# Spreading the weight loads over the first attention pairs, and storing the last tokens in pieces

## Chip, cores, metric

The kernel runs on one core of a Trainium2 chip. The metric is the device time of one execution in microseconds (us). Engines are named as in the profile: PE is TensorE (matmuls; PEld its weight loads), DVE is VectorE, ACT ScalarE, POOL GpSimd, SP SyncE. A name with a q (SPq, POOLq, ACTq) is the queue from which an engine issues DMAs.

## The reference

Attention without a mask, and behind it a two-layer MLP with a leaky ReLU, on 8 batches of 12 heads, 448 tokens of 64 numbers each:

```python
scores = scale * np.matmul(q, k.transpose(0, 1, 3, 2))
attn = np.exp(scores - max); attn = attn / np.sum(attn, axis=-1)
x = np.matmul(attn, v).transpose(0, 2, 1, 3).reshape(3584, 768)
h = x @ w_in            # 768 x 2048
out = np.maximum(0.01 * h, h) @ w_out   # 2048 x 768
```

Inputs and output are float32; the kernel multiplies in bf16.

## The kernel before

**Units.** Two heads of one batch make a pair; there are 48 pairs, six for a batch. For each pair `load` (line 97) brings q, k and v from memory by three DMAs on SP's queue (224 KB each), and `cast` (lines 108 to 110) turns them to bf16, on POOL for all pairs but the first. `transposes` turns q and k so that the head dimension lies on partitions: eight PE matmuls against an identity (line 169) and one DVE copy (line 172). For pairs from `NPE` = 12 on `dma_transposes` does it by a DMA transpose on SP (line 157). `scores(u, c)` multiplies q with a quarter of the keys (line 181) for both heads, `expo` takes the exponential on ACT (line 190), and `pv(u, j)` multiplies with v for one head (line 199); v has a column of ones, so the sum comes along, and DVE divides (lines 206 and 207) into `x`. `x_transposes` turns x into `xT`, on PE (lines 220 and 221) for pairs below 9 and by a DMA transpose from pair 9 on.

**MLP tiles.** Tokens are cut at multiples of 128 into eight tiles, one ending at or below the end of each batch: tile 0 has 384 tokens, others 384 or 512. `mlp(i)` is a generator of groups. First 16 groups of six matmuls each with w_in (line 250), each evicted by ACT with a leaky ReLU (line 254). Then two groups for each 128 tokens, one for each half of 384 columns, of 16 matmuls with w_out (line 268), evicted by a DVE copy into `o` (line 272). When the second half is done, `store` writes 128 rows by two DMAs on SP (line 232); they are two since rows of the output are interleaved by four in a batch.

**Order.** The order is written out by hand, and each engine runs its instructions in it. `first(u)` is the step of one of the first six pairs: scores and exponentials of pair u, heads of pair u - 1, transposes of pair u + 1, cast of pair u + 3, load of pair u + 5. From then on attention goes in clusters of three score quarters with what belongs to them (`cluster(g)`), put between groups of the MLP by `catch_up`. In tile 0 that is by the share of columns done; cluster 8, the first, goes ahead of all groups. Tile i waits for the attention of its own batch.

**Weights.** `load_w` issues w_in and w_out from POOL's queue in four pieces each (line 123), a DMA that also converts to bf16. The first piece of w_in is issued behind the casts of pair 0, ahead of those of pairs 1 and 2; the others from `first(2)` on:

```python
load_w({2: 1, 3: 2, 4: 2, 5: 2}.get(u, 0))
```

**Buffers.** PSUM has three score buffers of two banks (`ps_s`) and two others (`ps_g`) that transposes, heads and MLP groups share. Raw loads have five buffers, casts four. Each DMA of SP's queue waits for the landing of the one issued eight before it.

Of the kernel before, what the change touches and what calls it, by code (L numbers as in the profile page):

```python
# [9 lines left out]
F32 = mybir.dt.float32  # L10
BF16 = mybir.dt.bfloat16
# [5 lines left out]
def kernel(  # L17
# [53 lines left out]
    NQ = 4  # L71
# [31 lines left out]
    def cast(u, by=(nc.gpsimd.tensor_copy,) * 3):  # L103
        if u >= NU:
            return
        fq, fk, fv = raw.pop(u)
        qk_sb[u] = cast_pool.tile([SC, 2, NSC, 2, D], BF16, name="qkb")
        by[0](qk_sb[u][:, 0].rearrange("p so h d -> p h so d"), fq)  # L108
        by[1](qk_sb[u][:, 1].rearrange("p so h d -> p h so d"), fk)  # L109
        by[2](v_sb[u % NV][:, :, :, :D], fv)  # L110
# [21 lines left out]
    def warm_up(n):  # L132
        for _ in range(n):
            ps = ps_g.tile([P, 512], F32, name="mm", tag="g")
            nc.tensor.matmul(ps, warm[:, :P], warm, start=True, stop=True)  # L135
# [19 lines left out]

    def turn(dst, src):
        nc.sync.dma_start_transpose(out=dst.rearrange("p (c s) -> p c s", s=SC), in_=src)
# [5 lines left out]
    def transposes(u):  # L163
        if u >= min(NPE, NU):
            return
        tr = ps_g.tile([P, 2, S], BF16, name="tr", tag="g")
        for i in range(2):
            for so in range(NSC):
                nc.tensor.transpose(  # L169
                    tr[:, i, ts(so, SC)], qk_sb[u][:, i, so], ident[:SC, :SC]  # L170
                )
        nc.vector.tensor_copy(qkT[u % NQ][:, :QL], tr.rearrange("p i s -> p (i s)"))  # L172

    sc_t = {}

    def scores(u, c):
        ps = ps_s.tile([P, 2, 512], F32, name="sc")
        t = qkT[u % NQ]
        sc_t[u, c] = ps
        for j in range(2):  # L180
            nc.tensor.matmul(  # L181
                ps[:, j, :S],
                t[j * D:(j + 1) * D, S + c * SC:S + c * SC + P],
                t[j * D:(j + 1) * D, :S],
                start=True, stop=True,
            )
# [24 lines left out]
    def x_transposes(u):  # L211
        b, hp = divmod(u, HP)
        at = b * S % NX
        dst = xT[:, hp, at:at + S]
        if u >= NPE - 3:
            turn(dst, x_t.pop(u).rearrange("p so h d -> p (so h d)"))
            return
        tr = ps_g.tile([P, 2, S], BF16, name="tr", tag="g")
# [5 lines left out]
    def store(o, t0):  # L224
# [17 lines left out]
    def mlp(i):  # L242

        n = cuts[i + 1] - cuts[i]
        at = cuts[i] % NX
        h = h_pool.tile([P, MD, 4 * P], BF16, name="h")
        for m in range(MD):
            ps = ps_g.tile([P, 4 * P], F32, name="mm", tag="g")
            for kk in range(KD):
                nc.tensor.matmul(  # L250
                    ps[:, :n], w_in_sb[:, kk, ts(m, P)], xT[:, kk, at:at + n],
                    start=(kk == 0), stop=(kk == KD - 1),
                )
# [4 lines left out]
        todo = [(c, w) for c in range(n // P) for w in range(2)]  # L258
        if i == 0:
            todo.sort(key=lambda cw: cw[1])  # L260
        o = {}
        for c, w in todo:
            settle()
            if c not in o:
                o[c] = o_pool.tile([P, DM], F32, name="o")
            ps = ps_g.tile([P, 4 * P], F32, name="mm", tag="g")
            for m in range(MD):
                nc.tensor.matmul(  # L268
                    ps[:, :NW], h[:, m, ts(c, P)], w_out_sb[:, m, ts(w, NW)],
                    start=(m == 0), stop=(m == MD - 1),  # L270
                )
            nc.vector.tensor_copy(o[c][:, ts(w, NW)], ps[:, :NW])  # L272
            if w == 1:
                store(o.pop(c), cuts[i] + c * P)
            yield MD * NW


    def first(u):

        scores(u, 0)  # L280
        scores(u, 1)
        expo(u, 0)
        if u == 0:
            warm_up(4)
        expo(u, 1)
        if u >= 2:
            x_transposes(u - 2)
        if u >= 1:
            pv(u - 1, 0)
        load(u + 5)  # L290
        load_w({2: 1, 3: 2, 4: 2, 5: 2}.get(u, 0))
        if u + 1 < HP:
            transposes(u + 1)
        scores(u, 2)
        scores(u, 3)
        expo(u, 2)
        expo(u, 3)
        cast(u + 3)
        if u >= 1:
            pv(u - 1, 1)  # L300


    def cluster(g):
        t, r = divmod(g, 4)
        u = 3 * t
        chunks = [divmod(4 * u + 3 * r + x, NSC) for x in range(3)]
        chunks = [(a, c) for a, c in chunks if a < NU]
        heads = [[(u - 1, 0)], [(u - 1, 1)], [(u, 0), (u, 1)], [(u + 1, 0), (u + 1, 1)]][r]
        heads = [(a, j) for a, j in heads if HP <= a < NU]
        turned = {0: u - 2, 2: u - 1, 3: u}.get(r)  # L310
        if turned is not None and HP <= turned < NPE - 3:
            x_transposes(turned)
        if len(heads) > 1:
            pv(*heads.pop(0))
        for a, c in chunks:
            scores(a, c)
        for a, c in chunks[:2]:
            expo(a, c)
        late.extend(chunks[2:])
        for a, j in heads:  # L320
            pv(a, j)
            if j == 1 and a >= NPE - 3:
# [12 lines left out]
    u = HP - 1  # L335
    pv(u, 0)
    x_transposes(u - 1)
    pv(u, 1)
    transposes(HP)
    x_transposes(u)  # L340


    begin = [8 * (i + 1) + 3 for i in range(B)]
    begin[0] = 8
    for i in range(B):
        work = list(range(begin[i], begin[i + 1])) if i + 1 < B else []
        n = cuts[i + 1] - cuts[i]
        total = MD * KD * n + n // P * MD * DM
        used, done = 0, 0
        lead = 1 if i == 0 else 0  # L350

        def catch_up():
            nonlocal done
            while done < len(work) and used * (len(work) - lead) >= total * (done + 1 - lead):
                settle()
                cluster(work[done])
                done += 1

        catch_up()
        for step in mlp(i):  # L360
            used += step
            catch_up()


# [28 lines left out]
```

The softmax here doesn't subtract the row's maximum and nothing guards it: scores larger than these inputs give would overflow.

## Time and profile before

| | |
|---|---|
| median of 11 runs | 426.0 us (423.9 to 428.72) |
| the profiled execution | 425.32 us, span 423.5 us |
| PE / ACT / DVE / POOL busy | 96% / 54% / 24% / 21% |
| DMA, mean | 150 GB/s, 63.66 MB |
| mean granted clock of PE | 0.994 |

The span runs from the first to the last instruction; the execution has 1.8 us around it. Busy shares are means over stages that differ: the first six pairs, where there is no MLP work yet, the seven tiles with attention between their groups, and the last tile alone. Times in the views are in us from the start of the span. "Idle before, releaser" in brackets at the end of a line is how long the engine stood before that instruction and whom it waited for.

### The profile page before, as it was taken

The page shows a single profiled execution, that of the slowest core. Times are in us where ns is not written, and L with a number is a line of the kernel's source. Part 1 is how long each engine was busy: PE and PEld are TensorE (multiplying, and loading weights), DVE is VectorE, ACT ScalarE, POOL GpSimd, SP SyncE. Part 2 cuts the span into 40 slices and gives each one's busy share as a digit, 9 for nine tenths or more (in the row PEclk, how much of TensorE's full clock was granted, in tenths as well). Part 3 has the DMA queues.
Part 4 walks back from the last instruction along what each step waited for, and adds up shares of the span by engine and source line. Part 5 has one row for each costly group of instructions (what it writes and reads, how often), then busy time and mean ns, then how long its engine had stood idle before and what let it go on. Part 6 is the DMA issues. An engine that isn't in the chain of part 4 may idle for free.

```text
span 423.5 us, 9000 instructions
## 1 busy us (share of the span) xinstructions
PE 408.4 (96%) x3731; PEld 234.3 (55%) x3731; DVE 99.7 (24%) x271; ACT 228.3 (54%) x322; POOL 91.0 (21%) x168
## 2 busy tenths in 40 slices
PE   8979999979999999999999999999999999999995
PEld 3645556544556656554565656654465666654562
DVE  1642323310132212221132212321032211320021
ACT  4957664556724684467634486456652577214200
POOL 5494320530311211131131213131120200000000
PEclk9989999999999999999999999999999999999999
DMA  9999999994465947777465785759275420230022
GB/s 225 259 249 245 249 250 217 248 231 99 105 161 155 208 111 184 185 155 178 97 153 146 199 146 132 198 155 208 60 171 149 118 56 15 58 86 2 0 76 74
DMA packets 98505, 63.66 MB, mean 150 GB/s; under 512 B 55456, under 2 KB 94880, under 8 KB 98464
## 3 DMA queue, kind: packets, MB, share of 16 engines
q1 hardware_dynamic: 90928, 56.56, 55.7%
q0 software_dynamic: 7296, 6.29, 9.2%
q8 instruction: 29, 0.48, 0.5%
q10 hardware_dynamic: 240, 0.23, 0.2%
q14 instruction: 12, 0.10, 0.1%
HBM read 45.61 MB, written 11.01 MB: 134 GB/s over the span
## 4 chain that ended last, share of the span: by engine, by line
PE 90%; DMA 6%; DVE 1%; SPq 1%; ACT 1%; POOL 0%; issue 0%; ACTq 0%
PE mm L250 34%; PE mm L268 34%; PE pv L199 12%; PE sc L181 9%; DMA fv<-in_v_dram 3%; DMA xT<-x 2%; DMA fq<-in_q_dram 1%; DVE o L272 1%; SPq L97 1%; DVE x L207 1%; PE tr L169 0%; ACT e L190 0%; DVE rec L206 0%; POOL w_in_sb L123 0%; SPq L232 0%
## 5 line engine op out<-in xcount | busy, mean ns | idle before, releaser
L190 ACT ACTIVATE e<-sc 112x896 bf16<-112x896 f32 x192 | 164.4, 918 | 104.7 <-PE sc L181 104.3
L250 PE MATMUL mm<-xT,w_in_sb 128*128 128x384 bf16 (+1 forms) x768 | 150.4, 353 | 2.9 <-DMA xT<-x 2.2
L268 PE MATMUL mm<-w_out_sb,h 128*128 128x384 bf16 x896 | 150.5, 326 | 0.6 <-DVE x L207 0.3
L268 PEld LDWEIGHTS <-h 128*128 128x128 bf16 x896 | 85.8, 98 | 55.4 <-DVE x L207 0.5
L250 PEld LDWEIGHTS <-w_in_sb 128*128 128x128 bf16 x768 | 72.9, 98 | 68.8 <-issue 2.7
L254 ACT ACTIVATE h<-mm 128x384 bf16<-128x384 f32 (+1 forms) x128 | 69.6, 544 | 61.9 <-PE mm L250 61.8
L110 POOL CAST v<-fv 112x512 bf16<-112x512 f32 x48 | 29.6, 616 | 209.1 <-PE pv L199 189.1
L199 PEld LDWEIGHTS <-e 112*128 112x128 bf16 x1536 | 57.1, 98 | 30.2 <-issue 17.9
L199 PE MATMUL pv<-v,e 112*128 112x65 bf16 x1536 | 66.4, 195 | 2.6 <-ACT e L190 1.2
L272 DVE COPY o<-mm 128x384 f32<-128x384 f32 x56 | 31.2, 558 | 133.7 <-PE mm L268 133.7
L206 DVE RECIPROCAL rec<-pv 112x4 f32<-112x4 f32 x96 | 17.5, 183 | 160.5 <-PE pv L199 160.4
L181 PE MATMUL sc<-qkT 64*128 64x448 bf16 x384 | 49.5, 357 | 0.7 <-DVE qkT L172 0.4
L207 DVE TENSOR_TENSOR x<-pv,rec 112x256 bf16<-112x256 f32 x96 | 40.8, 425 | 3.3
L108 POOL CAST qkb<-fq 112x512 bf16<-112x512 f32 x47 | 28.9, 615 | 26.2 <-DMA qkT<-qkb 12.7
L109 POOL CAST qkb<-fk 112x512 bf16<-112x512 f32 x47 | 28.9, 614 | 10.0 <-DMA fk<-in_k_dram 9.9
L181 PEld LDWEIGHTS <-qkT 64*128 64x128 bf16 x384 | 13.6, 94 | 19.5 <-issue 10.4
L172 DVE COPY qkT<-tr 128x896 bf16<-128x896 bf16 x12 | 7.4, 619 | 10.6 <-PE tr L169 10.6
L169 PE MATMUL tr<-ident,qkb 112*128 112x112 bf16 x96 | 7.6, 223 | 1.5 <-POOL qkb L108 1.4
L169 PEld LDWEIGHTS <-qkb 112*128 112x128 bf16 x96 | 5.6, 102 | 3.7 <-POOL qkb L108 1.7
L135 PE MATMUL mm<-warm 128*128 128x512 bf16 x15 | 5.8, 531 | 1.2 <-DVE warm L130 1.2
L221 DVE COPY xT<-tr 128x448 bf16<-128x448 bf16 x9 | 3.5, 389 | 7.2 <-PE tr L220 7.2
L220 PE MATMUL tr<-ident,x 112*128 112x112 bf16 x36 | 3.3, 214 | 0.5 <-DVE x L207 0.3
(17 smaller groups left out, 14.9 us busy)
## 6 DMA issues: line engine op xcount, KB each, us to landing
fq<-in_q_dram SPq DMA_DIRECT2D x48, 224.0 KB, 3.8
fv<-in_v_dram SPq DMA_DIRECT2D x48, 224.0 KB, 4.4
fk<-in_k_dram SPq DMA_DIRECT2D x47, 224.0 KB, 3.9
w_in_sb<-in_moe_w_in_dram POOLq DMA_DIRECT2D x4, 768.0 KB, 15.0
w_out_sb<-in_moe_w_out_dram POOLq DMA_DIRECT2D x4, 768.0 KB, 34.9
out_dram<-o SPq DMA_DIRECT2D x8, 336.0 KB, 3.1
out_dram<-o SPq DMA_DIRECT2D x8, 288.0 KB, 2.6
out_dram<-o SPq DMA_DIRECT2D x8, 240.0 KB, 3.4
```

What stands on the lines that cost most here:

```text
L108: by[0](qk_sb[u][:, 0].rearrange("p so h d -> p h so d"), fq)
L109: by[1](qk_sb[u][:, 1].rearrange("p so h d -> p h so d"), fk)
L110: by[2](v_sb[u % NV][:, :, :, :D], fv)
L181: nc.tensor.matmul(ps[:, j, :S], t[j * D:(j + 1) * D, S + c * SC:S + c * SC + P], t[j * D:(j + 1) * D, :S], start=True, stop=True,)
L190: nc.scalar.activation(e[:, :, c, :], sc_t.pop((u, c))[:SC, :, :S], AX.Exp, scale=scale)
L199: nc.tensor.matmul(ps[:, qc, :], e[:, at:at + P], vt[:, j, c, :], start=(c == 0), stop=(c == NSC - 1),)
L206: nc.vector.reciprocal(rec, ps[:SC, :, D:])
L207: nc.vector.tensor_mul(x_t[u][:, :, j, :], ps[:SC, :, :D], rec.to_broadcast([SC, NSC, D]))
L250: nc.tensor.matmul(ps[:, :n], w_in_sb[:, kk, ts(m, P)], xT[:, kk, at:at + n], start=(kk == 0), stop=(kk == KD - 1),)
L254: nc.scalar.activation(h[:, m, :n], ps[:, :n], AX.Prelu, alpha=0.01)
L268: nc.tensor.matmul(ps[:, :NW], h[:, m, ts(c, P)], w_out_sb[:, m, ts(w, NW)], start=(m == 0), stop=(m == MD - 1),)
L272: nc.vector.tensor_copy(o[c][:, ts(w, NW)], ps[:, :NW])
```

## The change

In the order of the code:

- The first piece of w_in is no longer issued ahead of pair 1's casts; `first(0)` to `first(5)` issue 1, 1, 1, 2, 2 and 1 pieces.
- k of pair 0 is cast in two halves, by ACT and POOL. For pair 0, `transposes` uses a tile and a DVE copy for q and one for k. The two warm-up matmuls behind them are taken out.
- `NPE` is 14: pairs 12 and 13 are turned on PE as well. The border for x stays at pair 9, with a name of its own, `NXP`.
- In a cluster, PE's transposes of q and k stand ahead of the scores instead of at the end, and in such a cluster no head is put ahead of the scores. x's transposes on PE stand behind the exponentials.
- After pair 5, the transposes of x (pairs 4 and 5) and of pair 6 use score buffers, and those of pair 4 come ahead of pair 5's heads.
- In tile 0 the eleven clusters come after 2, 4, ... 22 groups.
- In the last tile, the last group is made as two of 192 columns, and the last 128 tokens are stored after each of their three column pieces, 16 rows from ACT's queue and 112 from SP's.

```diff
-    cast(0, (nc.vector.tensor_copy, nc.scalar.copy, nc.gpsimd.tensor_copy))
-    load_w()
+    def cast_k(o, i):
+        nc.scalar.copy(o[:, 0], i[:, 0])
+        nc.gpsimd.tensor_copy(o[:, 1], i[:, 1])
+    cast(0, (nc.vector.tensor_copy, cast_k, nc.gpsimd.tensor_copy))
...
-    NPE = 12
+    NXP = 9
+    NPE = 14
...
+    def turn_tile(idle):
+        if idle:
+            return ps_s.tile([P, 2, S], BF16, name="tr", tag="sc")
+        return ps_g.tile([P, 2, S], BF16, name="tr", tag="g")
...
-        tr = ps_g.tile([P, 2, S], BF16, name="tr", tag="g")
-        for i in range(2):
...
+        for parts in ((0,), (1,)) if u == 0 else ((0, 1),):
+            tr = turn_tile(idle)
+            for i in parts:
...
-            nc.sync.dma_start(out=dst[so, p:p + n], in_=o[done:done + n, :])
+            queues.pop(0).dma_start(out=dst[so, p:p + n, cols], in_=o[done:done + n, cols])
...
+        if i == B - 1:
+            todo[-1:] = [(c, slice(w, w + NW // 2)) for c, w in ((n // P - 1, NW), (n // P - 1, NW + NW // 2))]
...
-            if w == 1:
-                store(o.pop(c), cuts[i] + c * P)
+            t0 = cuts[i] + c * P
+            if i == B - 1 and c == n // P - 1:
+                store(o[c], t0, w, (nc.scalar, nc.sync))
+            elif w.stop == DM:
+                store(o.pop(c), t0)
...
-        load_w({2: 1, 3: 2, 4: 2, 5: 2}.get(u, 0))
+        load_w({0: 1, 1: 1, 2: 1, 3: 2, 4: 2, 5: 1}.get(u, 0))
...
-        if turned is not None and HP <= turned < NPE - 3:
-            x_transposes(turned)
-        if len(heads) > 1:
+        if turn_q < NPE:
+            transposes(turn_q)
+        elif len(heads) > 1:
             pv(*heads.pop(0))
...
+        if HP <= turn_x < NXP:
+            x_transposes(turn_x)
         for a, j in heads:
...
-        transposes({3: u + 3, 0: u + 1, 1: u + 2}.get(r, NU))
...
     transposes(0)
-    warm_up(2)
     for u in range(HP):
         first(u)
-    u = HP - 1
-    pv(u, 0)
-    x_transposes(u - 1)
-    pv(u, 1)
-    transposes(HP)
-    x_transposes(u)
+    x_transposes(HP - 2, True)
+    pv(HP - 1, 0)
+    pv(HP - 1, 1)
+    transposes(HP, True)
+    x_transposes(HP - 1, True)
...
+    early = [2, 4, 6, 8, 10, 12, 14, 16, 18, 20, 22]
...
-            while done < len(work) and used * (len(work) - lead) >= total * (done + 1 - lead):
+            while done < len(work) and (
+                groups >= early[done] if i == 0 else used * len(work) >= total * (done + 1)
+            ):
```

More of the change, by code (lines that the diff above doesn't have):

```diff
@@ L161, in dma_transposes, with transposes @@
             turn(qkT[u % NQ][:, :QL], qk_sb[u].rearrange("p i so h d -> p (i so h d)"))
-    def transposes(u):
+    def turn_tile(idle):
+        if idle:
+            return ps_s.tile([P, 2, S], BF16, name="tr", tag="sc")
+        return ps_g.tile([P, 2, S], BF16, name="tr", tag="g")
+    def transposes(u, idle=False):
         if u >= min(NPE, NU):
             return
-        tr = ps_g.tile([P, 2, S], BF16, name="tr", tag="g")
-        for i in range(2):
[L168 to L172, printed above, removed]
+        for parts in ((0,), (1,)) if u == 0 else ((0, 1),):
+            tr = turn_tile(idle)
+            for i in parts:
+                for so in range(NSC):
+                    nc.tensor.transpose(
+                        tr[:, i, ts(so, SC)], qk_sb[u][:, i, so], ident[:SC, :SC]
+                    )
+            at = slice(parts[0], parts[-1] + 1)
+            nc.vector.tensor_copy(
+                qkT[u % NQ][:, :QL].rearrange("p (i s) -> p i s", i=2)[:, at], tr[:, at]
+            )
     sc_t = {}
     def scores(u, c):
-        ps = ps_s.tile([P, 2, 512], F32, name="sc")
+        ps = ps_s.tile([P, 2, 512], F32, name="sc", tag="sc")
         t = qkT[u % NQ]
@@ L209, in pv, with x_transposes @@
         )
-    def x_transposes(u):
+    def x_transposes(u, idle=False):
         b, hp = divmod(u, HP)
@@ L214, in x_transposes @@
         dst = xT[:, hp, at:at + S]
-        if u >= NPE - 3:
+        if u >= NXP:
             turn(dst, x_t.pop(u).rearrange("p so h d -> p (so h d)"))
             return
-        tr = ps_g.tile([P, 2, S], BF16, name="tr", tag="g")
+        tr = turn_tile(idle)
         for so in range(NSC):
@@ L221, in x_transposes, with store @@
         nc.vector.tensor_copy(dst, tr[:, 0, :])
-    def store(o, t0):
+    def store(o, t0, cols=slice(0, DM), queues=(nc.sync, nc.sync)):
+        queues = list(queues)
         done = 0
@@ L256, in mlp @@
             yield KD * n
-        todo = [(c, w) for c in range(n // P) for w in range(2)]
+        halves = [slice(0, NW), slice(NW, DM)]
+        todo = [(c, w) for c in range(n // P) for w in halves]
         if i == 0:
-            todo.sort(key=lambda cw: cw[1])
+            todo.sort(key=lambda cw: cw[1].start)
+        if i == B - 1:
+            todo[-1:] = [(c, slice(w, w + NW // 2)) for c, w in ((n // P - 1, NW), (n // P - 1, NW + NW // 2))]
         o = {}
@@ L266, in mlp @@
             ps = ps_g.tile([P, 4 * P], F32, name="mm", tag="g")
+            nw = w.stop - w.start
             for m in range(MD):
                 nc.tensor.matmul(
-                    ps[:, :NW], h[:, m, ts(c, P)], w_out_sb[:, m, ts(w, NW)],
+                    ps[:, :nw], h[:, m, ts(c, P)], w_out_sb[:, m, w],
                     start=(m == 0), stop=(m == MD - 1),
                 )
-            nc.vector.tensor_copy(o[c][:, ts(w, NW)], ps[:, :NW])
-            if w == 1:
-                store(o.pop(c), cuts[i] + c * P)
-            yield MD * NW
+            nc.vector.tensor_copy(o[c][:, w], ps[:, :nw])
+            t0 = cuts[i] + c * P
[3 more added lines that the diff above has]
+                store(o.pop(c), t0)
+            yield MD * nw
     def first(u):
@@ L309, in cluster @@
         heads = [(a, j) for a, j in heads if HP <= a < NU]
-        turned = {0: u - 2, 2: u - 1, 3: u}.get(r)
-        if turned is not None and HP <= turned < NPE - 3:
-            x_transposes(turned)
-        if len(heads) > 1:
+        turn_q = {3: u + 3, 0: u + 1, 1: u + 2}.get(r, NU)
+        turn_x = {0: u - 2, 2: u - 1, 3: u}.get(r, 0)
+        if turn_q < NPE:
+            transposes(turn_q)
+        elif len(heads) > 1:
             pv(*heads.pop(0))
@@ L319, in cluster @@
         late.extend(chunks[2:])
+        if HP <= turn_x < NXP:
+            x_transposes(turn_x)
         for a, j in heads:
             pv(a, j)
-            if j == 1 and a >= NPE - 3:
+            if j == 1 and a >= NXP:
                 x_transposes(a)
@@ L348 @@
         total = MD * KD * n + n // P * MD * DM
-        used, done = 0, 0
-        lead = 1 if i == 0 else 0
+        used, done, groups = 0, 0, 0
         def catch_up():
             nonlocal done
-            while done < len(work) and used * (len(work) - lead) >= total * (done + 1 - lead):
+            while done < len(work) and (
+                groups >= early[done] if i == 0 else used * len(work) >= total * (done + 1)
+            ):
                 settle()
@@ L361 @@
             used += step
+            groups += 1
             catch_up()
```

## The prediction

> **What bounds the kernel now.** I read the totals first, then the stages by window, then the timeline where TensorE (PE) is not full. The totals:
>
> ```profile
> PE 408.4 (96%) x3731; PEld 234.3 (55%) x3731; DVE 99.7 (24%) x271; ACT 228.3 (54%) x322; POOL 91.0 (21%) x168
> ...
> DMA  9999999994465947777465785759275420230022
> ```
>
> PE is the bound over the whole, and the DMA engines are full for the first nine slices (95 us), then no more. So the stages are read apart (start:end, length, then busy time by engine in the order PE, PEld, DVE, ACT, POOL, the granted clock, and DMA):
>
> ```profile
> 6.50:29.35 22.85, 19.49 (x271) 11.40 (x271) 10.49 (x29) 19.80 (x24) 16.19 (x26) 0.93 1.15 259
> 29.35:33.80 4.45, 3.35 (x60) 2.42 (x61) 2.37 (x7) 0.65 (x2) 3.71 (x6) 1.00 1.18 246
> 33.80:60.40 26.60, 25.19 (x265) 15.41 (x263) 6.80 (x19) 20.68 (x34) 9.22 (x15) 1.00 1.20 248
> 60.40:84.80 24.40, 23.95 (x258) 14.77 (x259) 8.28 (x22) 11.75 (x15) 6.58 (x12) 1.00 1.19 234
> 84.80:140.00 55.20, 53.04 (x450) 28.98 (x448) 11.10 (x31) 28.42 (x40) 10.83 (x19) 1.00 0.63 155
> 140.00:397.50 257.50, 257.23 (x2292) 146.99 (x2289) 54.84 (x154) 144.45 (x209) 42.44 (x73) 1.00 0.54 128
> ```
>
> From 140 us to the last tile PE loses 0.3 us: nothing is to be had there, and the edit does not reach it. The losses are before 90 us and after 418.5 us. In the first six pairs (6.5 to 29.35) ACT's 24 exponentials and PE run side by side at some 3.3 us for a pair, with one hole, and a second one stands at tile 1:
>
> ```profile
> 20.42 0.62 POOL L110 CAST v<-fv 112x512 bf16<-112x512 f32 x1 [2.80 <-DMA fv<-in_v_dram]
> 22.47 1.10 PE L169 MATMUL tr<-ident,qkb 112*128 112x112 bf16 x8 [1.36 <-POOL qkb L108]
> 24.16 5.19 ACT L190 ACTIVATE e<-sc 112x896 bf16<-112x896 f32 x6 [2.08 <-PE sc L181]
> 88.22 4.26 PE L250 MATMUL mm<-xT,w_in_sb 128*128 128x512 bf16 x19 [2.16 <-DMA xT<-x]
> ```
>
> Pair 4's v landed 11.5 us after its issue, POOL stood on its cast, pair 5's casts stood behind it, then PE's transposes, then ACT. The cause is the first w_in piece: the DMA queues of two windows, 9 to 11 us and 30 to 33 us (packets, MB, share):
>
> ```profile
> q1 hardware_dynamic: 575, 0.55, 112.1%
> ...
> q0 software_dynamic: 382, 0.37, 73.5%
> q1 hardware_dynamic: 384, 0.36, 44.5%
> ```
>
> Alone, the loads (queue q1) move 288 packets a us, so one load (240 packets) takes 0.83 us; beside weights (q0) both move some 125, one for one, so a load takes 1.95 us. Near 55 us, with the shorter rows of w_out, it is 145 each, 1.65 us a load.
>
> **What the Trainium skill says.** "DMA: Bandwidth & Descriptors", section SWDGE vs HWDGE vs iDMA: GpSimd's DMAs and SP's sit in different queues of each engine, which the engine serves in turn; the 382 to 384 above agree. Its section Anatomy of one DMA has a fixed part and one by size, the fixed mostly the receipt of the last write; the last two stores agree in kind (48 KB 1.7 us, 336 KB 2.8 us from issue to landing: 1.5 us and 0.0038 us a KB). "TensorE: Matmul & The Clock Gate", Part 1, ties slow matmuls to an idle array: after the hole at 21 us eight transposes take 1.10 us against 0.56, and the clock of that stage is 0.93, the only one under 1.00.
>
> **The change, part by part**, against the profiled execution (425.3 us, span 423.5; the median of the 11 runs, 426.0, is 0.7 above it).
>
> *Start.* k of pair 0 is cast in halves on ACT and POOL, q's and k's transposes have their own tile and copy, two warm-up matmuls go. ACT's cast of 512 columns took 0.62 us, half is some 0.4 by ACT's forms of 384 and 512 columns (0.49, 0.60); POOL's half is not shown, between 0.3 and its whole 0.61. The last copy before the scores shrinks from 0.62 (896 columns) to 0.39 (448, line 221). First scores at 6.1 instead of 6.5: **-0.4** (0 to -0.6).
>
> *w_in later and spread.* Piece 0 was issued at 6.2 us and its packets ran from 11.7 to 18.1. Now POOL issues it behind pair 2's v cast, which waits for a landing at 10.6: issue at 11.2, packets, 4.4 to 5.5 us later as with pieces 0 and 1, from about 16. Until then loads come every 0.83 us: pair 4's v at 15.5 (was 20.4), pair 5's q at 16.4 and k at 17.6, wanted by PE at 20. The 2.08 us hole closes: **-2.1** (at least -1.0). POOL's further issues (0.82 to 0.95 each, one or two a pair) and casts (1.85 a pair) are 2.7 to 3.6 us a pair; pairs that carry two issues are not urgent.
>
> *End of batch 0.* The last exponential ends near 26.9 (was 29.35). Before, the two heads and the transposes of pairs 4, 5 and 6 shared two buffers: waits of 0.54, 0.34 and 0.16, W_in's first group 4.4 us after it, with 1.2 us of cluster 8 already done, 3.2 net. Now transposes use score buffers: head, head, eight transposes, four, first group: 0.6 + 0.6 + 0.5, then DVE's 0.8 behind the second head, 2.2. **-1.0** (-0.3 to -1.2). W_in starts at 29.2.
>
> *Weights thereafter.* Once packets run they run without a break: w_in at 6.25 us a piece (landings of before 33.4, 39.7, 45.9), w_out at 7.1 (53, 60, 67, 73.4). From 16: 22, 28.5, 35, 41, then 48, 55, 62, 69. Each is ahead of its use (group 16 at 62, the last piece near 73), so they cost nothing themselves.
>
> *But loads pay.* From 16 us on every load takes 1.95 us instead of 0.83. q of pair 5 is the 16th in order; k of pair 8 is ten on: 16.4 + 19.5 = 35.9, less a part of the first, say 35.5; cast and seen at 36.3. The changed kernel transposes pair 8 in cluster 9, now ahead of that cluster's scores, after four groups: 29.2 + 4 x 0.98 + cluster 8 (1.2) = 34.3. **+2.2** (0.5 to 5); queued behind are the scores, then ACT. Later: pair 9 seen at 42.4 for 43.5, pair 10 at 47.3 for 48.4, pair 11 at 52.3 for 52.3, then pairs 12 and 13 in good time.
>
> *Clusters every two groups, pairs 12 and 13 on PE.* Two sets of eight transposes at 0.5: **+1.0**. Two fewer DMA transposes, the first of which held SP for 6.9 us and landed 15.1 us on; PE did not wait for it, so 0. The order of the rest changes what PE waits for: in 33.8 to 84.8 its short waits (0.38, three of 0.34, 0.45) are 1.9. Heads that now stand side by side keep some 0.3 each, and ACT is tighter: 2 x 0.49 + 3 x 0.9 = 3.7 us per cluster against PE's 3.2 in the first two and 3.8 to 4.7 after: **-0.7** (-1.3 to +0.8).
>
> *Tile 1's wait.* x of pair 11 left by DMA at 81.77 and took 6.42 us; PE wanted it at 86.06. In even steps of two groups, there lie two groups (5.2) and cluster 18 (1.9) behind that head instead of one group and the cluster: 2.6 us more lead against 2.16 missing: **-2.2** (0 to -2.2). Stores now in front of it on SP are those of group 19, done by then.
>
> *Tail.* The last DVE copy halves: 0.56 to some 0.37 (between 0.18 for four columns and 0.56 for 384). The 16-row store (0.4 of SP's time) goes to ACT's queue, idle since 398, and the last one has 84 KB instead of 336: 1.5 + 0.3 instead of 2.8. -0.2 - 0.4 - 1.0, and +0.1 for 192-column matmuls (16 take 1.3 to 1.4 us by the 384- and 65-column ones, 0.163 and 0.039 each): **-1.4** (-0.5 to -1.8).
>
> Sum: -0.4 - 2.1 - 1.0 + 2.2 + 1.0 - 0.7 - 2.2 - 1.4 = -4.6: 420.7 for such an execution, **421.4** as median.
>
> **Rivals.** (1) *More wait for loads, still faster*: k of pair 8 three us later, as if packets of w_in began at once: 424.4. For it: every load is slowed from the first weight packet on. Against: both delays of before were over 4 us. (2) *x still late at tile 1*, since q, k, v loads and stores fill the queue: -2.4, 423.6. (3) *No wait for pair 8*, ACT holding the clusters anyway: -6.8, 419.2. (4) *Slower: pair 8 starves cluster 9.* The gains without that wait are 6.8; it decides from 8.1 us on, a k landing at 41.7, or 2.5 us a load instead of 1.95. At 2.7 it lands at 43.4 and the time is 429. Against: 113 to 128 packets a us in every window from 12 to 36 us in which both queues ran. (5) *Nothing gained*: the hole of 2 us only moves from pair 4 to pair 8 and the x wait stays: near 426.
>
> **Chances.** The forecast 0.6; (1) 0.15, (2) 0.08, (3) 0.06, (4) 0.06, (5) 0.05. About 0.3% (1.3 us) is what a measurement of this kernel can tell. A part of (1) falls within it: faster 0.87, same 0.07, slower 0.06. The range 418.5 to 424.5 takes in (2), (3) and most of (1).
>
> **What would show it.** Right: no ACT hole near 22 us; W_in's first matmul near 29; one PE wait of 1 to 4 us for pair 8's casts near 35; no wait for xT at tile 1, which starts near 83; last matmul near 415.4, and 3.4 us from there to the end instead of 4.9. Wrong: PE waits for casts in several clusters, a wait for w_in or w_out, or an xT wait near 84.

## The result, and the profile after

The changed kernel takes **419.91 us** (median of 12 runs) against 425.21 for the kernel before (median of 47 runs that stood beside it and beside the experiments). The ratio is **0.9866**, with a 95% interval of 0.984 to 0.9893. The ratios here and below leave out the executions more than 1.5% above the fastest of their kernel (here one of the 12, 2068.81 us, and one of the 47, 594.44 us), and they are not quotients of the medians. The forecast was 421.4, in a range of 418.5 to 424.5.

The profiled execution of the changed kernel took 417.91 us with a span of 416.1, near the lowest of its own runs (417.84 to 422.03 without the one named). Against the profiled execution of before (425.32) that is -7.4 us, against -5.3 for the medians. Why these two differ is one of the things that the experiments look into.

The totals of the changed kernel (first part and the DMA line of the second part of its page):

```profile
PE 407.3 (98%) x3761; PEld 236.3 (57%) x3761; DVE 101.4 (24%) x275; ACT 227.5 (55%) x322; POOL 91.9 (22%) x169
...
DMA  8999999972666748575465756758275440230032
```

PE has 30 more matmul instructions and 1.1 us less of busy time. Of the slices of DMA the second to the eighth are full; before it was the first nine. By stages (start:end, length, then busy time of PE, PEld, DVE, ACT, POOL, the granted clock, DMA share, GB/s):

```profile
6.10:27.00 20.90, 18.48 (x280) 11.39 (x280) 11.07 (x31) 19.58 (x24) 16.99 (x27) 1.00 1.15 266
29.00:60.00 31.00, 30.38 (x355) 19.14 (x352) 10.31 (x27) 25.37 (x39) 11.26 (x18) 1.00 1.20 248
60.00:83.00 23.00, 22.78 (x213) 13.76 (x210) 7.38 (x19) 8.80 (x12) 9.58 (x16) 1.00 1.17 256
83.00:140.00 57.00, 57.00 (x503) 31.80 (x500) 11.95 (x34) 31.45 (x45) 10.49 (x19) 1.00 0.61 157
```

The stage of the first six pairs ends at 27 us instead of 29.35 and has the full clock instead of 0.93. From 29 to 60 us PE loses 0.62 us, from 60 to 83 us 0.22, and behind that nothing: the 2.2 us at tile 1 are gone. The timeline shows each place (start, length, engine, line, operation, count; in brackets the idle time before it and its releaser):

```profile
5.62 0.76 DVE L185 COPY qkT<-tr 128x448 bf16<-128x448 bf16 x2 [0.87 <-PE tr L181]
8.95 17.86 ACT L205 ACTIVATE e<-sc 112x896 bf16<-112x896 f32 x22 [0.38 <-PE sc L196]
28.94 2.12 PE L266 MATMUL mm<-xT,w_in_sb 128*128 128x384 bf16 x12
34.01 0.86 PE L181 MATMUL tr<-ident,qkb 112*128 112x112 bf16 x8
81.16 5.34 PE L266 MATMUL mm<-xT,w_in_sb 128*128 128x512 bf16 x24
75.03 1.24 SPq L162 DMA_TRANSPOSE xT<-x  x1
412.60 0.36 DVE L293 COPY o<-mm 128x192 f32<-128x192 f32 x1 [0.96 <-PE mm L289]
```

In the order of the lines: the two copies of pair 0 stand back to back. ACT runs the last 22 of its 24 exponentials without a break, where before it stood 2.08 us ahead of the last six. W_in's first matmul is at 28.94. Pair 8's eight transposes run as one block of 0.86 us; the other whole blocks of eight take 0.56, and the 0.3 us more are a wait for the cast of k. Tile 1 starts at 81.16 with no wait for xT, whose DMA left at 75.03. The last copy took 0.36 instead of 0.56. The stores of the changed kernel's last piece (queue, form, count, size, us from issue to landing):

```profile
out_dram<-o SPq DMA_DIRECT2D x2, 84.0 KB, 1.8
...
out_dram<-o ACTq DMA_DIRECT2D x2, 12.0 KB, 1.9
```

So the time splits into four places:

| place | before | after | difference |
|---|---|---|---|
| last exponential of batch 0 ends at | 29.35 | 26.81 | -2.5 |
| from there to W_in's first matmul | 4.4 | 2.1 | -2.3 |
| from W_in's first matmul until PE starts tile 1, its wait for xT included | 53.2 | 52.2 | -1.0 |
| last matmul to the end of the span | 5.0 | 3.5 | -1.4 |

Cluster 8 (1.2 us of PE) has moved from the second row into the third, and the transposes of pairs 12 and 13 (1.0) have come into the third too; without them the second row is -1.1 and the third -3.2. Between tile 1's first matmul and the last matmul, the wait for xT left out, the kernel before takes 331.5 us and the changed one 331.4.

### The profile page after: what moved, and what is told of

The parts are those of the page before. It is cut to its first block, busy times and chain, and to the rows that moved or that the text cites. A ratio compares the mean times of both kernels' runs of the same rounds, so it can differ in the third digit from the quotient of the medians.

```text
span 416.1 us, 9068 instructions
## 1 busy us (share of the span) xinstructions
PE 407.3 (98%) x3761; PEld 236.3 (57%) x3761; DVE 101.4 (24%) x275; ACT 227.5 (55%) x322; POOL 91.9 (22%) x169
## 4 chain that ended last, share of the span: by engine, by line
PE 87%; DMA 9%; POOL 2%; DVE 1%; issue 0%; SPq 0%
PE mm L289 35%; PE mm L266 32%; PE pv L214 11%; PE sc L196 8%; DMA fv<-in_v_dram 5%; DMA fk<-in_k_dram 4%; POOL w_in_sb L123 1%; POOL v L110 1%; POOL qkb L108 0%; POOL qkb L109 0%; DVE o L293 0%; PE tr L181 0%; POOL w_out_sb L123 0%; DVE x L222 0%; PE tr L235 0%
## 5 line engine op out<-in xcount | busy, mean ns | idle before, releaser
L289 PE MATMUL mm<-w_out_sb,h 128*128 128x384 bf16 (+1 forms) x912 | 150.2, 323 | 0.5 <-DVE x L222 0.2
L289 PEld LDWEIGHTS <-h 128*128 128x128 bf16 x912 | 87.0, 98 | 54.6 <-issue 0.5
L214 PEld LDWEIGHTS <-e 112*128 112x128 bf16 x1536 | 56.7, 98 | 26.0 <-issue 16.3
L293 DVE COPY o<-mm 128x384 f32<-128x384 f32 (+1 forms) x57 | 31.4, 551 | 133.5 <-PE mm L289 133.5
L221 DVE RECIPROCAL rec<-pv 112x4 f32<-112x4 f32 x96 | 17.5, 183 | 151.6 <-PE pv L214 151.2
L108 POOL CAST qkb<-fq 112x512 bf16<-112x512 f32 x47 | 28.9, 615 | 12.5 <-DMA fq<-in_q_dram 10.5
L185 DVE COPY qkT<-tr 128x896 bf16<-128x896 bf16 (+1 forms) x15 | 8.8, 590 | 15.8 <-PE tr L181 15.8
L181 PE MATMUL tr<-ident,qkb 112*128 112x112 bf16 x112 | 8.7, 219 | 0.5 <-POOL qkb L109 0.3
L181 PEld LDWEIGHTS <-qkb 112*128 112x128 bf16 x112 | 7.0, 100 | 2.7 <-POOL qkb L109 1.0
```

The lines of the kernel that those rows point to most:

```text
L214: nc.tensor.matmul(ps[:, qc, :], e[:, at:at + P], vt[:, j, c, :], start=(c == 0), stop=(c == NSC - 1),)
L289: nc.tensor.matmul(ps[:, :nw], h[:, m, ts(c, P)], w_out_sb[:, m, w], start=(m == 0), stop=(m == MD - 1),)
L293: nc.vector.tensor_copy(o[c][:, w], ps[:, :nw])
```

## The experiments

All are edits of the changed kernel. The medians of the kernel before beside them were 425.61 us (unchanged, weights as before, spacing as before, tail as before), 424.95 (weights one step later, pair 8 later, `NPE` 12, `NPE` 12 with the old spacing) and 425.33 (the other four).

### The changed kernel again

No edit; a second profiled execution.

> The changed kernel once more, as the reference of this group and for a second profile: the profiled execution of the first was at the fast end of its own runs (span 416.1, median 419.9). Theory (the saving is before 82 us and at the end, and the scatter comes from there too): ratio to before 0.985 to 0.989; if the profile falls on a slower execution, the missing 2 us lie ahead of tile 1 (a late load, PE idle before 85 us), and the stretch from tile 1's first matmul to the last matmul is again 331.4 us within 0.3. Rival (the scatter is a slower clock over the whole execution): that stretch is longer by 1 us or more.

Measured: 420.4 us, ratio 0.9892 (0.983 to 0.9954). This execution's span was 418.4, 2.3 longer than the first one's, and the timeline says where:

```profile
35.08 0.37 PE L181 MATMUL tr<-ident,qkb 112*128 112x112 bf16 x4 [0.78 <-POOL qkb L108]
36.96 0.37 PE L181 MATMUL tr<-ident,qkb 112*128 112x112 bf16 x4 [1.51 <-POOL qkb L109]
...
83.43 5.34 PE L266 MATMUL mm<-xT,w_in_sb 128*128 128x512 bf16 x24
```

PE waited 0.78 us for the cast of pair 8's q and 1.51 for that of its k, 2.3 together; tile 1 started 2.27 later. From tile 1's first matmul to the last one it is 331.4 us again, so the rival, a slower clock over the whole execution, is out. **The wait that was forecast is there in this execution and was missing in the first, but for 0.3 us.** The two differ in the loads. The DMA queue of the loads between 9 and 11 us, ahead of all weight packets (packets, MB, share), in the first execution:

```profile
q1 hardware_dynamic: 619, 0.58, 111.3%
```

and in the second:

```profile
q1 hardware_dynamic: 532, 0.51, 112.3%
```

310 packets a us in one, 266 in the other. Over the profiled executions of those kernels that leave the order of the loads and the weights alone, the rate, the first packet of the weights' queue (q0), POOL's cast of pair 8's q and the start of tile 1 go together, nearly in one order:

| kernel | packets a us, 9 to 11 us | first weight packet | cast of q of pair 8 starts | tile 1 starts |
|---|---|---|---|---|
| changed | 310 | 16.2 | 32.00 | 81.16 |
| end of batch 0 as before | 285 | 16.6 | 32.31 | 81.82 |
| tail as before | 270 | 17.5 | 34.30 | 83.42 |
| again | 266 | 17.6 | 34.40 | 83.43 |
| pairs 8 and 11 later, tail in four pieces | 264 | 17.7 | 34.63 | 83.48 |
| `NPE` 12 | 256 | 18.3 | 35.20 | 90.94 |
| start as before | 252 | 18.6 | 35.08 | 85.54 |
| pairs 8 and 11 later | 246 | 18.5 | 35.36 | 84.14 |

Tile 1 of "start as before" and of `NPE` 12 is later than its row, for reasons told there. A load of 240 packets costs 0.77 to 0.98 us at these rates and 1.95 us beside the weights. The number of loads at each price is the same in all eight: ahead of the first weight packet q1 has moved 3900 to 4010 packets, 16.3 to 16.7 loads. So a slow start makes the first sixteen loads later, and with them the weights and every load behind. What sets the rate in an execution the profile does not show, and no run set it on purpose.

### The weights issued as before

```diff
     cast(0, (nc.vector.tensor_copy, cast_k, nc.gpsimd.tensor_copy))
+    load_w()
...
-        load_w({0: 1, 1: 1, 2: 1, 3: 2, 4: 2, 5: 1}.get(u, 0))
+        load_w({2: 1, 3: 2, 4: 2, 5: 2}.get(u, 0))
```

> The changed kernel with the weight pieces issued as before: the first piece of w_in behind pair 0's casts, the others from pair 2's step. Theory (the first piece's packets delay pairs 3 to 5 and open ACT's hole): pair 4's v lands near 20 us instead of 15.5, ACT idle 2 us near 22 us, W_in's first matmul at 31.4 instead of 28.9, ratio to the changed kernel +2.5 us (about 0.6%); no wait for pair 8's casts. Rival (loads only pay later, the total DMA work is the same): the 2.5 us come back in tile 0, since loads of pairs 8 to 11 are then earlier, and the time differs by less than 0.7 us.

Measured: 421.17 us, ratio 0.9901 (0.9865 to 0.9937): 0.8 us above the unchanged kernel of that comparison, with overlapping intervals. Pair 4's v is late again, as the theory had it (cast at 20.28; 20.42 in the kernel before, 15.91 in the changed one). But ACT does not stand near 22 us; it waits earlier:

```profile
20.28 0.62 POOL L110 CAST v<-fv 112x512 bf16<-112x512 f32 x1 [0.82 <-DMA fv<-in_v_dram]
...
9.68 3.34 ACT L206 ACTIVATE e<-sc 112x896 bf16<-112x896 f32 x4 [1.48 <-PE sc L197]
13.50 3.53 ACT L206 ACTIVATE e<-sc 112x896 bf16<-112x896 f32 x4 [0.48 <-PE sc L197]
17.31 11.51 ACT L206 ACTIVATE e<-sc 112x896 bf16<-112x896 f32 x14 [0.28 <-PE sc L197]
```

The first of these waits comes from k of pair 1, which POOL waited for until 8.30 (7.57 in the changed kernel), ahead of any weight packet (the first is at 11.8); behind it PE's clock is at 0.66 from 11 to 16 us. PE and ACT were late by then, and pair 5's transposes followed at 22.91 (20.80 in the changed kernel) without a wait. This profile shows the late landing, but not the hole, and how much of what follows is the weights' work stays open.

W_in starts at 30.95, 2.0 us later than with the edit, but there is no wait for pair 8 behind it, and tile 1 starts at 83.79 against 83.43 (again) and 81.16 (first execution). So most of what the later weights win in the first pairs, the loads of pair 8 can take back: by these three profiles this part of the change is worth between 0.4 and 2.6 us. Only the first piece is issued earlier here, and the others up to one piece later; PE waits 1.20 us for w_out at 74.19.

### The weights one step later

```diff
-        load_w({0: 1, 1: 1, 2: 1, 3: 2, 4: 2, 5: 1}.get(u, 0))
+        load_w({1: 1, 2: 1, 3: 2, 4: 2, 5: 2}.get(u, 0))
```

> The changed kernel with every weight piece one pair's step later (the first behind pair 3's casts, then 1, 1, 2, 2, 2). Theory (tile 0 is bound by the packets that all loads and weights share, so a wait only moves): weight packets start some 2.6 us later, three more loads come at the full rate, PE's wait for pair 8's casts (2.3 us in the second run of the changed kernel) goes, but the last w_out piece lands 2.6 us later and PE waits 1 to 2 us for it in tile 0's groups 18 to 20; tile 1 starts within 1 us of the changed kernel, the time is the same within 0.8 us. Rival (weights have slack behind and only the loads are short): no wait for w_out, time 1.5 to 2.3 us less than the changed kernel.

Measured: **423.21 us**, ratio 0.9947 (0.9921 to 0.9974), some 3 us worse than the changed kernel. The waits for pair 8 fall to 0.42, as the theory had it, but the end of tile 0 stands:

```profile
76.63 2.19 PE L289 MATMUL mm<-w_out_sb,h 128*128 128x384 bf16 x8 [3.73 <-DMA w_out_sb<-in_moe_w_out_dram]
```

PE waits 3.73 us for w_out, its clock is at 0.68 from 76.6 to 82 us (these eight matmuls take 2.19 us instead of 1.46), and tile 1 starts at 87.76. The place was forecast, the size was not: the wait was put at 1 to 2 us and the time within 0.8 us of the changed kernel, since the slack of w_out was taken to be larger than it is and a drop of the clock was left out.

### The weights one pair earlier

```diff
     cast(1)
+    load_w()
     cast(2)
...
-        load_w({0: 1, 1: 1, 2: 1, 3: 2, 4: 2, 5: 1}.get(u, 0))
+        load_w({0: 1, 1: 1, 2: 2, 3: 2, 4: 1}.get(u, 0))
```

> The changed kernel with every weight piece of w_in earlier by one pair (the first behind pair 1's casts, then 1, 1, 2, 2, 1). Theory (early loads are the scarce part; every pair's step of weights moved ahead delays the loads behind it by one to one and a half loads at double time): packets of w_in start near 13.5 us, pair 8's k lands 1.5 to 3 us later, PE waits 2 to 5 us for casts of pairs 5 to 9, none for w_out; 1 to 3 us slower than the changed kernel. With the later start (3.7 us of wait for w_out) that makes the place of the change one between two losses. Rival (the start of the weights does not matter within one pair): the same time within 0.7 us.

Measured: **423.1 us**, ratio 0.9953 (0.9933 to 0.9973), 2.5 to 3 us worse. From its timeline:

```profile
32.65 0.37 PE L182 MATMUL tr<-ident,qkb 112*128 112x112 bf16 x4 [1.41 <-POOL qkb L109]
...
38.41 0.37 PE L182 MATMUL tr<-ident,qkb 112*128 112x112 bf16 x4 [1.50 <-POOL qkb L109]
...
39.39 3.65 PE L267 MATMUL mm<-xT,w_in_sb 128*128 128x384 bf16 x12
```

With the 0.78 for pair 8's q, PE waits 3.7 us for casts of pairs 7 and 8, and then twelve matmuls take 3.65 us where they take 2.12 elsewhere: the granted clock from 39 to 44 us is 0.66. There is no wait for w_out. Together the last two runs show that **the change stands between two losses**, late loads on one side and late w_out on the other, each some 3 us at one step's distance.

### Spacing of the clusters as before

```diff
-                groups >= early[done] if i == 0 else used * len(work) >= total * (done + 1)
+                used * (len(work) - 1) >= total * done if i == 0 else used * len(work) >= total * (done + 1)
```

> The changed kernel with tile 0's eleven clusters placed by the share of columns, as before (after 0, 4, 7, 10, 13, 16, 18, 19, 20, 21, 22 groups). Theory (the spacing gives x of pair 11 its lead): the last head of pair 11 is again followed by one group and one cluster only, PE waits 1.5 to 2.5 us for xT in tile 1's first group, +2.2 us, less up to 0.5 for looser exponentials. Rival (the wait came from the DMA queues being full of two more transposes and weights until 73 us): no wait over 0.5 us, time as the changed kernel within 0.7 us.

Measured: 420.9 us, ratio 0.9876 (0.9822 to 0.993): not to be told from the changed kernel. The xT wait did **not** come back:

```profile
73.22 1.46 PE L289 MATMUL mm<-w_out_sb,h 128*128 128x384 bf16 x8 [1.64 <-DMA w_out_sb<-in_moe_w_out_dram]
80.96 1.19 SPq L162 DMA_TRANSPOSE xT<-x  x1
84.49 5.40 PE L266 MATMUL mm<-xT,w_in_sb 128*128 128x512 bf16 x24
```

The DMA left at 80.96, 4.8 us before PE wanted x of pair 11 in tile 1's first group; it landed in 4.6 us instead of the 6.42 of before. The old spacing alone is not the cause of that wait. At 73.22 PE waits 1.64 us for w_out, which neither profile of the changed kernel shows.

### `NPE` back to 12

```diff
-    NPE = 14
+    NPE = 12
```

> The changed kernel with pairs 12 and 13 turned by DMA again. Theory (sixteen PE transposes cost 1.0 us and what they relieve is hidden): PE work in tile 0 falls by 1.0 us, the DMA transpose of pair 12 holds SP for several us and lands 10 us or more later, pair 12's scores stand at 66.5 us and would wait for it; net between -1.0 and +2.0, and x of pair 11 keeps its lead of 7 us, no wait at tile 1. Rival (the two DMA transposes made x late at tile 1, not the spacing): an xT wait of 1 us or more comes back.

Measured: **427.48 us**, ratio 1.0056 (1.0038 to 1.0074): slower than the kernel before, and the interval leaves out 1. Its timeline:

```profile
62.92 7.00 SPq L162 DMA_TRANSPOSE qkT<-qkb  x1
...
74.91 1.30 PE L196 MATMUL sc<-qkT 64*128 64x448 bf16 x6 [6.53 <-DMA qkT<-qkb]
```

The DMA transpose of pair 12's q and k was issued at 62.92, held SP for 7.0 us, and PE's scores of pair 12 waited 6.53 us for it until 74.91, 12 us after the issue. The even spacing asks for pair 12 after 18 groups, the old one after 20: in the next run, with the old spacing, such a DMA left at 62.82 and its reader stood at 75.60. **Pairs 12 and 13 on PE are what makes the spacing possible.**

### `NPE` back to 12 and the spacing as before

Both edits together.

> The changed kernel with both undone: tile 0's clusters by the share of columns and pairs 12 and 13 turned by DMA. With the spacing alone undone x landed 4.6 us after its issue against 4.8 us of lead. Theory (lead and landing time meet; two more DMA transposes make it land later, 6.4 us as before): PE waits 1 to 2.5 us for xT in tile 1's first group. Rival (the landing time has nothing to do with them): no such wait, or under 0.3 us.

Measured: 422.34 us, ratio 0.993 (0.9904 to 0.9956). Now the wait at tile 1 is back, in a smaller size:

```profile
32.93 5.56 PE L266 MATMUL mm<-xT,w_in_sb 128*128 128x384 bf16 x24
...
82.55 1.26 SPq L162 DMA_TRANSPOSE xT<-x  x1
...
87.52 4.26 PE L266 MATMUL mm<-xT,w_in_sb 128*128 128x512 bf16 x19 [1.18 <-DMA xT<-x]
```

There is no 6.5 us wait. x of pair 11 was ready at 81.53, but SP, with stores and loads back to back from 78.70 on, sent it at 82.55; it landed in 4.9 us. With the old spacing alone it was ready at 80.93, left at 80.96 and landed in 4.6. So most of the difference is SP's queue, which the two DMA transposes had set back. By these executions, one of each kernel, the wait for xT needs the old spacing and the two DMA transposes of q and k together; either part of the change is enough to remove it, and neither can be told as its sole cause. The line at 32.93 shows something else: PE had waited 1.27 and 0.83 us for pair 7, and these 24 matmuls take 5.56 us where they take 4.27 with the spacing alone undone.

### The end of batch 0 as before

```diff
-    x_transposes(HP - 2, True)
-    pv(HP - 1, 0)
+    pv(HP - 1, 0)
+    x_transposes(HP - 2)
     pv(HP - 1, 1)
-    transposes(HP, True)
-    x_transposes(HP - 1, True)
+    transposes(HP)
+    x_transposes(HP - 1)
```

> The changed kernel with the end of batch 0 in the old order and buffers (pair 5's first head, x of pair 4, second head, pair 6, x of pair 5, all in the two general buffers); cluster 8 stays behind two groups. Theory: W_in's first matmul stands 3.0 to 3.3 us after the end of the last exponential of pair 5 instead of 2.1, with PE waits of 0.3 to 0.6 us for x; but where loads are slow, PE then waits 1 us less for pair 8's casts, so that the time grows by 0 to 1.1 us. Rival (the stage's gain is kept in full): 1.0 us or more, and the wait for pair 8 unchanged.

Measured: 420.66 us, ratio 0.9883 (0.9848 to 0.9918). W_in's first matmul comes 3.3 us behind the last exponential (26.70 to 30.02) instead of 2.13, with four short waits of 0.60, 0.54, 0.34 and 0.16. Of these 1.2 us, 0.7 are left at tile 1 (81.82 against 81.16), and the time is not distinct from the changed kernel's: at 285 packets a us pair 8's casts were ready in time here. So at most part of this gain reaches tile 1 in these two profiles.

### The start as before

```diff
-    cast(0, (nc.vector.tensor_copy, cast_k, nc.gpsimd.tensor_copy))
+    cast(0, (nc.vector.tensor_copy, nc.scalar.copy, nc.gpsimd.tensor_copy))
...
-        for parts in ((0,), (1,)) if u == 0 else ((0, 1),):
+        for parts in ((0, 1),):
...
     transposes(0)
+    warm_up(2)
```

> The changed kernel with pair 0 as before: k cast whole on ACT, one tile and one DVE copy for q and k, the two warm-up matmuls back. Theory (in the changed kernel both copies came back to back, 0.76 us together against 0.62, since PE was still at its nine warm-up matmuls when q was cast): first scores within 0.2 us of the changed kernel, no difference in time. Rival (the predicted 0.4 us): scores 0.4 us later.

Measured: 420.78 us (a median of two runs), ratio 0.989 (0.9843 to 0.9938). Its first exponential is at 7.20 against 6.84 and 6.63 in the two executions with the edit, part of it because k landed later. From the start of k's cast on ACT it is 2.16 us here, 2.17 in the kernel before, and 2.06 and 1.79 in those two; in the twelve executions with the edit it is 1.79 to 2.06 but for one of 2.44, and 1.83 in the median. So the edit gains some 0.3 us behind k's landing, which is nearer to the rival than to the theory. In the time a few tenths can't be told. In this execution PE waited 0.77 and 1.61 us for pair 8, and then its clock fell to 0.71 for five us; window of 38.9 to 44 us:

```profile
38.90:44.00 5.10, 5.10 (x49) 2.86 (x48) 0.61 (x2) 3.74 (x6) 1.84 (x3) 0.71 1.18 246
```

### The tail as before

```diff
-            todo[-1:] = [(c, slice(w, w + NW // 2)) for c, w in ((n // P - 1, NW), (n // P - 1, NW + NW // 2))]
+            pass
...
-            if i == B - 1 and c == n // P - 1:
+            if False:
```

> The changed kernel with the last group and the last store whole, as before: 384 columns, 16 and 112 rows of 768 columns from SP's queue. Theory: from the last matmul to the end 4.9 us instead of 3.5, the last copy 0.56 us instead of 0.36, the last store 2.8 us to landing instead of 1.8 to 2.0; +1.4 us. Rival (a fixed receipt time dominates the store): +0.5 us or less.

Measured: 421.94 us, ratio 0.9923 (0.9897 to 0.995), 1.5 us above the unchanged kernel beside it. Its profile starts tile 1 at 83.42, that of the unchanged kernel (again) at 83.43, and the spans are 419.9 and 418.4: the 1.5 us lie behind that. Last matmul to end takes 5.1 us again. Its last stores:

```profile
out_dram<-o SPq DMA_DIRECT2D x1, 336.0 KB, 2.8
...
out_dram<-o SPq DMA_DIRECT2D x1, 48.0 KB, 1.7
```

### Pair 8 transposed one cluster later

```diff
-        turn_q = {3: u + 3, 0: u + 1, 1: u + 2}.get(r, NU)
+        turn_q = {3: u + 3, 0: u + 1, 2: u + 2}.get(r, NU)
```

> The changed kernel with the transposes of pairs 8 and 11 one cluster later (10 and 14 instead of 9 and 13), the last place before their scores. Theory (loads come at the pace that the DMA engines give, pair after pair): where loads are slow the wait for pair 8 goes, and PE waits for pairs 9 and 10 instead, since k of pair 10 lands near 47.3 us whatever PE does; gain 0.3 to 1.0 us. Rival (one late pair only): the whole 2.3 us come off, less 0.4 for heads that now stand side by side.

The edit moves pair 11 as well as pair 8. Measured: 420.62 us, ratio 0.9855 (0.9781 to 0.9929), four runs that show no difference from the changed kernel. The waits went elsewhere: 0.66 us for pair 7, 0.23 for pair 10, others shorter. Loads that are late as a whole are not mended by asking later for one of them.

### The last piece in two

Pairs 8 and 11 later as above, and the last 192 columns as two groups of 96, each stored on its own.

```diff
-            todo[-1:] = [(c, slice(w, w + NW // 2)) for c, w in ((n // P - 1, NW), (n // P - 1, NW + NW // 2))]
+            todo[-1:] = [(c, slice(w, w + NW // 2)) for c, w in ((n // P - 1, NW),)] + [(n // P - 1, slice(w, w + NW // 4)) for w in (NW + NW // 2, NW + 3 * NW // 4)]
```

> A candidate: the changed kernel with pairs 8 and 11 transposed one cluster later and the last piece of 192 columns made and stored as two of 96. Theory: the first gives 0.3 to 0.6 us where loads are slow; the last DVE copy takes 0.27 us instead of 0.36 and the last store has 42 KB instead of 84, 0.1 to 0.2 us less to landing: 0.4 to 0.9 us below the changed kernel, ratio to before 0.984 to 0.987. Rival (both at a floor: the store's receipt, the loads' pace): no difference, 0.986 to 0.989.

Measured: 419.94 us, ratio 0.9874 (0.9844 to 0.9904). In the profile the tail is 0.5 us shorter (3.0 from the last matmul to the end), by the copy and the store:

```profile
414.96 0.26 DVE L293 COPY o<-mm 128x96 f32<-128x96 f32 x1 [0.42 <-PE mm L289]
```

The last 42 KB took 1.5 to 1.6 us against 1.8 for 84 KB. The time is not to be told from the changed kernel's, so no version was found that beats it. Of all parts taken back one at a time, only the tail and `NPE` stand out of the scatter; what the others are worth is read from the profiles alone.

## Why the prediction was right, and where it was not

The time, the sign and nearly all the places were right. By its steps:

- **w_in later, -2.1: right.** The packets of w_in came from 16.2 us (forecast 16), pair 4's v was cast at 15.91 (forecast landing 15.5), the hole in ACT closed, and the last exponential came 2.5 us sooner. It is 2.1 from the hole, 0.1 from the start, and 0.3 from the six exponentials behind the hole, which took 5.19 us where six others take 4.87; the sum had that nowhere. The sum put the packets 4.4 to 5.5 us behind the issue; over all profiles it was 4.8 to 6.3, and what stayed the same was the number of loads ahead. Undoing this part did not show the hole again, for the reason told there.
- **End of batch 0, -1.0: right in the profile**: W_in started at 28.94 (forecast 29.2), 2.13 us behind the last exponential (forecast 2.2). Putting the old lines back moved tile 1 by 0.7.
- **Loads pay, +2.2: the right place, and a cost that comes and goes.** It was 2.3 us in the second execution and 0.3 in the first. The step took one rate of the loads alone (288 a us, from one profile of before) as a constant; it was between 246 and 310. Its own times, 36.3 against 34.3, give 2.0 and not 2.2. Rival 3 of the prediction ("no wait for pair 8") and its forecast are both true, each for some executions, though rival 3's reason, ACT holding the clusters anyway, was not what happened: the casts were nearly in time. This wait accounts for nearly all of the 2.3 us between the two profiles, and it fits the difference between -7.4 in the first profile and -5.3 in the medians: rival 3 had -6.8, and the second execution, 420.1 in all, is -5.2 against a forecast of -4.6. That the total came so near owes something to luck, since the wait hangs on a rate that the sum did not know to vary.
- **Pairs 12 and 13, +1.0, their two DMA transposes 0: the sum right, the zero only with its condition.** "PE did not wait for it" held for the old spacing. With the new one the DMA transpose would have cost 6.5 us; the prediction did not name the cover that the spacing takes away. Both are parts of one change, so the zero held in it.
- **Other short waits, -0.7: about right.** In the first execution tile 0 to tile 1 took 52.2 us against 51.06 with 2.1 of added work on PE (two sets of transposes, and cluster 8's 1.2 that before lay ahead): -1.0 with all waits for loads in it.
- **xT wait, -2.2: right in size, half right in cause.** The prediction credited the lead of the new spacing, 2.6 us. The lead came (issue at 75.03, tile 1 at 81.16), but with the old spacing and no DMA transposes of q and k on the queue the same DMA landed in 4.6 us instead of 6.42, and there was no wait either. The prediction left out that the two DMA transposes set SP's queue back.
- **Start, -0.4: about right behind k's landing, 0.1 in the first execution.** There the first scores came 0.08 us sooner (6.44 for 6.52), in the second 0.29. Counted from k's cast the edit gains some 0.3 us, as the experiment shows. The sum took one copy of 448 columns as what is left ahead of the scores (0.39). In the second execution that holds: k's transposes and q's copy were over together. In the first one q was cast by 4.75, but its transposes began at 5.00 and the eight took 0.95 us (0.75 in the second), so that k's copy ended only 0.08 us before the single copy of the kernel before did. The nine warm-up matmuls ahead of them may be why: in "end of batch 0 as before" q was cast by 4.57, and the transposes began at 5.00 all the same. No run took them away.
- **Tail, -1.4: right.** 1.4 by the profile, 1.5 by undoing it (the parts that the prediction names add up to -1.5). The section that it cites for the fixed part of a DMA is on DMAs that GpSimd issues; these stores left from SP and ACT, and their 1.5 us rest on the two stores measured.
- **w_out "costs nothing itself": right, with less to spare than it said.** One step later costs 3.73 us of waiting, and in "end of batch 0 as before" PE waits 0.17 us for it without any change to the weights.

On the clock the Trainium skill ("TensorE: Matmul & The Clock Gate", Part 1) puts the drop behind an idle window of about 3.4 us. Here the clock was down behind shorter waits in five executions: behind one of 1.36 us in the kernel before (0.53 from 22.4 to 26 us), behind two of 0.78 and 1.50 us (weights one pair earlier, 0.66), of 0.77 and 1.61 (start as before, 0.71) and of 1.27 and 0.83 (both edits together, 0.73 from 32.1 to 38.5 us), with four transposes between the two, and behind 0.87 us among shorter ones in "weights as before". In three others, the second of the changed kernel among them, it stayed full behind 0.65 to 0.78 and 1.46 to 1.51 us. The measurement decides that such waits can be enough. What tells these executions apart stays open; a drop costs 1.3 to 1.5 us (3.55 and 3.65 for twelve matmuls instead of 2.12), and no run took it away by itself. The 1.10 us that the prediction reads for eight slow transposes contain a wait of 0.23 us of their weight loads for the cast of k.

## What to carry to other kernels

When two queues share the DMA engines, moving the start of the one moves the loads in between from one price to the other (here six loads, between 0.8 and 1.95 us), so count how many loads stand before and behind the start, and look for the next consumer on both sides: the loads that get later, and the weights themselves. A zero in a sum is a zero under a cover: ask of each part whether another part of the same change takes it away, as the even spacing would have done with the DMA transposes. And take a second profile of the same kernel before you read a difference of 2 us between two executions as the work of an edit.

## What was not expected of the hardware

- With loads alone on the engines, the rate differed between executions, from 246 to 310 packets a us between 9 and 11 us.
- The first weight packet kept its place among the loads and not its delay. Where 11 loads had been issued ahead of the first weight piece (the kernel before and "weights as before"), it came when 10.5 to 10.7 loads' packets had been moved; with 14 ahead (one pair earlier) 13.7, with 17 (the change) 16.3 to 16.7, with 20 (one step later) 19.4. The delay behind the issue was 4.8 to 6.3 us.
- Where both queues ran, their packets stayed one for one (370 of the weights and 374 of the loads from 14 to 17 us, weights issued as before), as "DMA: Bandwidth & Descriptors", SWDGE vs HWDGE vs iDMA, has it for queues that are served in turn.
- A DMA transpose of pair 12's q and k, issued while loads and weights filled the DMA engines, held SP for 7.0 us and let its reader wait until 12 us after the issue (`NPE` 12); those for x at 75 and 81 us held it for 1.2.
- The clock of PE fell to between 0.66 and 0.73 for five to six us after 2.1 to 2.4 us of waiting in three executions, and did not in three others after 2.1 to 2.3 us.
